# A new order table for a fused attention and channel-mix kernel: batch 6's q turned later, batch 7's k and v loaded side by side

## The chip, the cores and the metric

The kernel runs on one core of a Trainium2 chip. The time is the device time of one execution in microseconds (us). The engines that matter are TensorE (PE, with its weight loads PEld), VectorE (DVE), ScalarE (ACT), GpSimd (POOL) and SyncE (SP); the last two do little here but issue DMAs.

## The reference

Eight batches (B=8) with eight heads (H=8), 576 tokens (S=576), head size 64, so 512 channels; the hidden size F of the channel mix is 1024. The attention has no softmax: keys and values are first contracted into a 64 by 64 matrix for each head.

```python
kv  = einsum('bhsd,bhse->bhde', k, v)
o   = einsum('bhsd,bhde->bhse', q, kv)
o   = o / sqrt(mean(o * o, axis=-1) + 1e-6) * g_norm        # per head
x   = o.transpose(0, 2, 1, 3).reshape(B, S, 512)
xp  = x moved down by one token, zeros first                # token shift
xk  = mu_k * x + (1 - mu_k) * xp
xr  = mu_r * x + (1 - mu_r) * xp
kk  = relu(xk @ w_k)                                        # 512 -> 1024
out = sigmoid(xr @ w_r) * ((kk * kk) @ w_v)                 # 1024 -> 512
```

## The kernel before

The whole program is driven by a written table, ORDER (from line 18): eight strings ("periods") of words. A loop at the end of the kernel takes the words one after the other and calls the function that belongs to each. So the table sets, for every engine and every DMA queue, the order of its instructions. Each engine works through its own words in that order, and waits where a word needs something that is not there yet. A word has a name, numbers, and two marks:

- The digits behind `=` are the PSUM banks (of eight) that the word's result takes. A word that takes a bank waits until the one that held it before has been read out.
- A `'` at the end puts the word's elementwise part on DVE instead of ACT.

The words, by what they do for batch b:

- `ld.n.b` loads k (n=0), v (1) or q (2). POOL issues it (`load`, L196). Ahead of a load POOL copies one element of each DMA transpose that is still listed (L195), so a load, and all that POOL does after it, waits until every transpose that stands ahead of it in the table has landed.
- `kv` contracts k with v on PE (L288), `kvo` and `kvs` take the result out. `qt`/`qto` turn q on PE (batches 1 and 2), `qd` turns it by a DMA transpose that SP issues (from batch 3 on, L303). `u` multiplies q with kv (L354 or L318).
- `sq` (ACT, L359), `red` (DVE, L363), `nw` (DVE, eight small steps of a Newton iteration, L372 to L385) and `mul` (DVE, L423 or L401) are the norm. `mul` reads the last of u and so frees the bank of `u`.
- For batches 1 to 3 `x` and `x0` turn the normed result on PE (L438) and `xo`, `x0o` take it out. For batches 4 to 7 a DMA transpose does it (`yd`, SP, L411), and `gx` multiplies by g.
- `wrap`, `dif`, `sc` (L604 on ACT, L606 on DVE) and `add` (DVE, L621) make xk and xr.
- `K` is a half of a hidden block, four matmuls of 288 columns (L634) and a relu (L626 on ACT, L628 on DVE); `Kp` is the same in other sizes. `ks` and `ksp` square (L642 on DVE).
- `R` (four matmuls of 512 columns, L666) with the sigmoid on ACT; `V` (four, L676), two of them for a tile of 128 tokens; `fin` multiplies both on DVE (L689) and lets SP issue two stores (L699). `L` is the last tile.
- Batch 0 has words of its own so that PE can begin early, by pieces: `kvc`, `kvco`, `qtc`, `qtco` (out of PSUM, L217 on ACT, L219 on DVE), `uc`, `sqc` (square, L501), `msc` (mean by a matmul, L507), `rsc` (root, ACT, L511), `mcc` (product, DVE, L515), `difh`, `dih` (L598), `fu` (scale and add in one, DVE, L610), and `Ka`, `Kz`: the hidden blocks in two halves of the contraction (L725), `Ka` with the first two channel groups, `Kz` with the other two. Batch 1's attention is done in halves (`kvh`, L525, `uh`, L543, `sqh`, `redh`, `mulh`, `xh`, `x0h`).
- `wm.n.m` issues n matmuls on zeros (L261) between other work.

The periods overlap neighbouring batches: while the matmuls of batch b's channel mix run, the attention of b+1 and the transfers of b+2 go on. SP works through its transposes and stores strictly in the order of the table, and so does POOL through its loads.

Of the kernel before, what the change touches and what calls it, by code (L numbers as in the profile page):

```python
# [32 lines left out]
    Kp.0.1.2=1 rsh.5.9.0 mulh.1.1.0 sc.0.1.0 Kp.0.1.3=4 Vq.0.1.0=2 Vq.0.0.0=1 mulh.1.0.0 mulh.2.0.0 qt.1.1=70
    mulh.0.1.0 mulh.0.0.0 xh.2.2.0=36 x0h.0=54 qto.1.1.0 ld.2.3 xho.2.2.0.1 qto.1.1.1' x0ho.0.1' Vq.0.1.1
    xh.0.2.0=04 sc.0.1.1 xho.2.2.0.0' kvh.1=73 xho.0.2.0.0' kvho.1.1' ksp.0.1.4.8' Vq.0.0.1 kvho.1.0 uh.0.1=60
    uh.1.1=37 xho.0.2.0.1 uh.2.1=4 x0ho.0.0 Vq.0.0.2 sqh.0.1.1 sqh.1.1.1 sqh.0.0.1 sqh.1.0.1 ld.0.3 sqh.2.0.1
    add.0.1.1 Vq.0.3.0=5 Vq.0.3.1 redh.5.9.1 redh.0.5.1 rsh.5.9.1 rsh.0.5.1 Vq.0.1.2 mulh.0.1.1 mulh.0.0.1
    mulh.1.0.1 mulh.2.0.1 Vq.0.3.2 Vq.0.3.3 mulh.1.1.1 Vq.0.0.3 xh.2.2.1=06 Vq.0.1.3 xho.2.2.1.1 xho.2.2.1.0'
    xh.0.2.1=34 xho.0.2.1.0 x0h.1=76 add.0.1.0 Vq.0.2.0=0 xho.0.2.1.1 Vq.0.2.1 dif.1.384.576 tab R.0.1=3
    x0ho.1.1' wrap.1 x0ho.1.0' R.0.3=4 dif.1.0.384 sc.1.0.2.384.576' sc.1.0.3.0.384' sc.1.0.0.384.576' ld.1.3  # L40
    sc.1.0.2.0.384' sc.1.0.1.384.576' R.0.0=6 Vq.0.2.2 sc.1.0.1.0.384 qt.2.1=73 qt.2.0=46 ld.2.4 sc.1.0.0.0.384
    sc.1.1.3 sc.1.0.3.384.576' qto.2.1.1 Vq.0.2.3 fin.0.3 fin.0.0 R.0.2=5 adda.1.0.384.576 sc.1.1.1' qto.2.1.0
    Kp.1.0.2=1 add.1.0.1.0.384 Kp.1.0.0=3 add.1.0.0.0.384 qto.2.0.1' sc.1.1.2 sc.1.1.0 qto.2.0.0' fin.0.1
    Kp.1.1.2=5 add.1.1.1 Kp.1.1.3'=6 Kp.1.1.1'=7 Kp.1.1.4=4 add.1.1.0 fin.0.2 Kp.1.1.5=1 kv.2=32 Kp.1.1.0=5
    kvo.2.1' kvo.2.0' R.1.5=6 u.2.2=4 u.2.1=71 ksp.1.1.2.4' ksp.1.1.0.2' u.2.0=02 sq.2.1.1 ksp.1.1.4.6' sq.2.2.0
    Kp.1.0.3'=3 sq.2.1.0 qd.3 sq.2.0.0 sq.2.0.1 R.1.8=5 red.2.0.5 R.1.4=6 Kp.1.0.1=3 red.2.5.9 nw.2.0.1 nw.2.1.2
    nw.2.2.3 Kp.1.1.6=5 nw.2.3.4 Kp.1.1.7=6 nw.2.4.5 nw.2.5.6 nw.2.6.7 R.1.7=3 nw.2.7.8 mul.2.1.0 mul.2.1.1
# [7 lines left out]
    K.2.1.0=7 ld.2.5 nw.3.0.1 nw.3.1.2 K.2.5.1=5 nw.3.2.3 sc.2.1.2' nw.3.3.4 K.2.3.0=3 nw.3.4.5 nw.3.5.6
    nw.3.6.7 K.2.6.0=7 nw.3.7.8 K.2.6.1=5 K.2.2.0=3 K.2.2.1=7 sc.2.1.0' K.2.7.1=5 V.1.8.0=3 mul.3.0.1
    ks.2.3 ks.2.7 K.2.0.0=7 ks.2.0 mul.3.0.0 mul.3.1.0 mul.3.2.0 mul.3.1.1 K.2.4.1=0 add.2.1.0 K.2.4.0=5 x0.3=12
    ld.1.5 add.2.1.1 x.3.0.4=67 V.1.8.1 ks.2.2 xo.3.0.4.1 ks.2.1' x0o.3.0' ks.2.5 ks.2.4 R.2.0=4 ks.2.6'
    xo.3.0.4.0' R.2.2=0 x0o.3.1' wrap.3 dif.3 sc.3.0.2 sc.3.0.1 ld.0.5 V.2.0.0=5 ld.2.6 sc.3.0.0 V.2.0.1
# [8 lines left out]
    sc.3.1.3' K.3.1.1'=1 K.3.0.1=0 K.3.2.1=4 K.3.3.0=5 add.3.1.1 kvo.5.0' K.3.6.1'=7 ks.3.7 ks.3.2 fin.2.3
    kvs.5.0' ks.3.0 K.3.3.1=0 V.2.1.0=3 kvs.5.1 ks.3.5 R.3.7=4 V.2.1.1 u.5.1=51 ks.3.6' u.5.0=67 fin.2.1 ks.3.1'
    sq.5.1.0 u.5.2=0 sq.5.2.0 sq.5.1.1 sq.5.0.0 ks.3.3' sq.5.0.1 R.3.6=2 R.3.8=4 red.5.0.5 R.3.5=3 V.3.7.0=2  # L70
    gx.4.0 red.5.5.9 nw.5.0.1 gx.4.1' nw.5.1.2 nw.5.2.3 nw.5.3.4 R.3.4=4 nw.5.4.5 nw.5.5.6 nw.5.6.7 V.3.7.1
    V.3.4.0=3 wrap.4 nw.5.7.8 ld.0.6 dif.4 sc.4.0.2 mul.5.0.1 sc.4.0.0 sc.4.1.1 sc.4.0.1 sc.4.0.3 mul.5.2.0
# [14 lines left out]
    nw.6.7.8 mul.6.1.0 mul.6.0.0 K.5.1.0=6 V.4.0.1 sc.5.1.2 ks.5.2' kv.7=36 mul.6.1.1 kvo.7.1 kvo.7.0 qd.7
    add.5.1.0 V.4.1.0=2 V.4.1.1 kvs.7.1 mul.6.0.1 K.5.4.0=4 K.5.4.1=6 kvs.7.0' V.4.2.1 K.5.1.1=3 u.7.0=74
    mul.6.2.0 sq.7.0.0 yd.6 ks.5.7' sq.7.0.1 fin.4.0 add.5.1.1 u.7.1=50 u.7.2=6 sq.7.2.0 sq.7.1.0 R.5.4=3
    fin.4.2 sq.7.1.1 R.5.5=1 fin.4.1 ks.5.1' red.7.5.9 ks.5.3' red.7.0.5 nw.7.0.1 R.5.6=2 nw.7.1.2 nw.7.2.3  # L90
    R.5.8=3 nw.7.3.4 nw.7.4.5 ks.5.6 V.5.7.0=1 ks.5.4 nw.7.5.6 nw.7.6.7 V.4.3.0=2 nw.7.7.8 V.5.5.0=3 V.5.7.1
# [750 lines left out]
```

## Time and profile before

| | us |
|---|---|
| runs | 197.79, 198.43, 198.27 |
| median | 198.27 |
| profiled execution | 197.78 |
| its span | 196.0 |

| engine | busy us | share of the span |
|---|---|---|
| PE | 185.6 | 95% |
| PEld | 111.0 | 57% |
| DVE | 156.9 | 80% |
| ACT | 138.0 | 70% |
| POOL | 29.9 | 15% |

The profile is one execution; the profiled execution's own time is 1.8 us longer than the span of its instructions. In a row of the timeline stand: start, length, engine, line, operation, what is written from what is read, sizes, how many were joined, and in brackets the idle time ahead of it with what ended it. In a row of the windows stand: the stretch and its length, then for PE, PEld, DVE, ACT and POOL the busy time (and the number of instructions), the granted clock of PE, the DMA share and GB/s. In a row of the waits stand: total idle, how many times, the longest. A row of the chain has start and length. A row of the DMA issues ends with the time from the issue to the landing in us.

### The profile page before, as it was taken

The numbers are of one execution on the slowest core, as the hardware profiler recorded it, in microseconds if no ns is written. First come the engines' busy times: TensorE is split into PE (matmuls) and PEld (weight loads), VectorE is DVE, ScalarE is ACT, GpSimd is POOL, SyncE is SP. The second block draws the span as 40 slices with busy tenths as digits, with TensorE's granted clock in tenths as the row PEclk, the third lists the DMA queues.
The fourth block names the chain that finished last, engine by engine and source line by source line (L and its number), as shares of the span: only waits on it lengthen the run. The fifth ranks groups of instructions, "written<-read, shape, count | busy, mean of one in ns | idle before, by whom it ended". The sixth has DMA issues, their size and how long they took to land.

```text
span 196.0 us, 5662 instructions
## 1 busy us (share of the span) xinstructions
PE 185.6 (95%) x2314; PEld 111.0 (57%) x2343; DVE 156.9 (80%) x343; ACT 138.0 (70%) x285; POOL 29.9 (15%) x50
## 2 busy tenths in 40 slices
...
GB/s 213 213 210 207 198 207 205 208 223 260 215 184 169 131 246 212 210 271 177 149 185 135 215 128 184 247 229 5 181 120 118 127 54 0 107 3 109 107 158 163
DMA packets 42958, 32.75 MB, mean 167 GB/s; under 512 B 23852, under 2 KB 37428, under 8 KB 42932
## 3 DMA queue, kind: packets, MB, share of 16 engines
...
q8 instruction: 18, 0.29, 0.6%
...
HBM read 33.56 MB, written 9.44 MB: 219 GB/s over the span
## 4 chain that ended last, share of the span: by engine, by line
PE 64%; DMA 24%; DVE 6%; issue 2%; POOL 1%; ACT 1%; SPq 0%; POOLq 0%
PE ps_v L676 25%; PE ps_km L634 18%; DMA in_v<-in_v_dram 12%; PE ps_r L666 11%; DMA qT__1999<-in_q 7%; DMA rt<-in_v_dram 4%; PE ps_km L725 2%; PE ps_u L318 2%; DVE y__1672 L423 1%; DVE ss__1584 L363 1%; PE ps_warm L261 1%; PE ps_kv L288 1%; PE ps_v L684 1%; PE ps_x L438 1%; POOL q L183 1%
## 5 line engine op out<-in xcount | busy, mean ns | idle before, releaser
L676 PE MATMUL ps_v<-wv_sb,sqk 128*128 128x512 bf16 x264 | 65.1, 379 | 1.1 <-issue 0.5
L634 PEld LDWEIGHTS <-wk_sb 128*128 128x128 bf16 x480 | 45.9, 98 | 16.4
L676 PEld LDWEIGHTS <-sqk 128*128 128x128 bf16 x280 | 26.5, 98 | 28.3
L666 PE MATMUL ps_r<-wr_sb,xr 128*128 128x512 bf16 x134 | 34.7, 379 | 0.6 <-issue 0.2
L666 PEld LDWEIGHTS <-xr 128*128 128x128 bf16 x144 | 13.8, 98 | 14.3 <-DVE xr L621 0.2
L626 ACT ACTIVATE rt<-ps_km 128x384 bf16<-128x384 f32 (+2 forms) x20 | 9.5, 497 | 3.6 <-PE ps_km L634 1.9
L261 PE MATMUL ps_warm<-zeros 128*128 128x512 bf16 x25 | 9.1, 477 | 1.2 <-DVE eps L224 1.2
L634 PE MATMUL ps_km<-xk__3390,wk_sb 128*128 128x288 bf16 x64 | 9.0, 286 | 0.1
L634 PE MATMUL ps_km<-xk__2431,wk_sb 128*128 128x288 bf16 x64 | 8.8, 286 | 0.0
L634 PE MATMUL ps_km<-xk__2693,wk_sb 128*128 128x288 bf16 x64 | 8.7, 286 | 0.0
L634 PE MATMUL ps_km<-xk__986,wk_sb 128*128 128x192 bf16 (+1 forms) x64 | 8.5, 286 | 0.0
L634 PE MATMUL ps_km<-xk__3236,wk_sb 128*128 128x288 bf16 x64 | 8.5, 286 | 0.0
L634 PE MATMUL ps_km<-xk__1886,wk_sb 128*128 128x288 bf16 x64 | 8.4, 286 | 0.0
L634 PE MATMUL ps_km<-xk__1544,wk_sb 128*128 128x288 bf16 x64 | 8.2, 286 | 0.0
L428 ACT ACTIVATE xT<-ps_x,cols 128x256 bf16<-128x256 bf16 (+3 forms) x9 | 5.0, 591 | 2.8 <-PE ps_x L438 2.8
L261 PEld LDWEIGHTS <-zeros 128*128 128x128 bf16 x28 | 3.1, 116 | 5.5 <-issue 3.4
L725 PE MATMUL ps_km<-xk__376,wk_sb 128*128 128x320 bf16 x32 | 5.0, 299 | 0.5 <-DVE xk__376 L621 0.5
L428 ACT ACTIVATE xT<-xT,cols 128x1152 bf16<-128x1152 bf16 x4 | 5.0, 1261 | 0.0
L642 DVE TENSOR_TENSOR sqk<-rt 128x768 bf16<-128x768 bf16 (+2 forms) x7 | 4.5, 666 | 0.4 <-ACT rt L626 0.3
L628 DVE TENSOR_SCALAR rt__3521<-ps_km 128x288 bf16<-128x288 f32 x2 | 0.9, 458 | 4.7 <-ACT rt__3513 L626 4.7
L669 ACT ACTIVATE sig__3696<-ps_r 128x512 bf16<-128x512 f32 x1 | 0.6, 597 | 5.4 <-PE ps_r L666 5.4
L604 ACT ACTIVATE m__2398<-dx__2396,cols 128x576 bf16<-128x576 bf16 x4 | 2.9, 764 | 2.0 <-DVE dx__2396 L598 2.0
...
## 6 DMA issues: line engine op xcount, KB each, us to landing
q<-in_q_dram POOLq DMA_DIRECT2D x3, 576.0 KB, 18.5
sq<-in_k_dram POOLq DMA_DIRECT2D x3, 576.0 KB, 6.7
qT<-in_v_dram POOLq DMA_DIRECT2D x3, 576.0 KB, 11.2
in_q<-in_q_dram POOLq DMA_DIRECT2D x3, 576.0 KB, 13.0
in_k<-in_k_dram POOLq DMA_DIRECT2D x3, 576.0 KB, 18.5
in_v<-in_v_dram POOLq DMA_DIRECT2D x3, 576.0 KB, 18.0
...
sqk<-in_k_dram SPq DMA_DIRECT2D x1, 576.0 KB, 3.8
```

What stands on the lines that cost most here:

```text
L183: nc.gpsimd.dma_start(out=x_in[name, 0][:, ms], in_=by_token(dram[name], 0)[:, ms])
L261: nc.tensor.matmul(ps, zeros[:, :128], zeros, start=True, stop=True)
L288: nc.tensor.matmul(ps[e][half(i), M, :], kb[half(e), 2 * M + i, tok(j)], vb[half(e), 2 * M + i, tok(j)], start=(j == 0), stop=(j == G - 1))
L318: nc.tensor.matmul(out_, qT_[half(r), b // 2, half(ct % 2)], kv_[half(r), 0 if r == i else 1, ct, :], start=True, stop=True)
L428: eng.activation(out=dst, in_=src, func=AF.Copy, scale=g_sb)
L604: eng.activation(out=out_, in_=in_, func=AF.Copy, scale=mu)
L626: eng.activation(out=dst, in_=ps, func=AF.Relu)
L634: nc.tensor.matmul(ps[:, n, :], wk_sb[:, cc, 128 * fc:128 * fc + 128], at[b]["xk"][:, cc, c0:c1], start=(cc == 0), stop=(cc == NHP - 1))
L642: eng.tensor_mul(out=sqk[:, fcs, o:o + n], in0=src, in1=src)
L666: nc.tensor.matmul(ps, xr[:, cc, 128 * t:128 * t + 128], wr_sb[:, cc, :], start=(cc == 0), stop=(cc == NHP - 1))
L676: nc.tensor.matmul(ps, sqk[:, fc, 128 * t:128 * t + 128], wv_sb[:, fc, :], start=(fc == 0), stop=(fc == NFC - 1))
L725: nc.tensor.matmul(ps[:, n, :], wk_sb[:, cc, 128 * fc:128 * fc + 128], at[0]["xk"][:, cc, c0:c1], start=(cc == 0), stop=(cc == NHP - 1))
```

## The change

Only ORDER is replaced, all of it; no function is changed. Every step of the old table is in the new one, with the same number of matmuls. What differs is the order, the banks, the split of the warm matmuls, and the engine of some elementwise steps: 21 scales go from ACT to DVE and 16 the other way, 18 relus and 17 back, 14 squares and 9 back. In the parts that the text speaks of:

- Batch 0: `uc.1` now stands behind `qtc.2.2`; `kvco.2` between the two first `rsc`; `qtco.3'` behind `mcc.1`; `sc.0.0.0` on DVE; other banks for `Ka`. Seven `Ka` words stand ahead of the first `Kz` word and not five. `Kz.0.5` stands behind batch 1's `x0h.0`.
- Loads: batches 3 and 7 in another order (v3 ahead of k3; q7, k7, v7), k of batch 6 together with v of batch 6 behind `yd.4`.
- Transposes: `qd.5` behind `kv.5` (it stood right behind the `u` words of batch 4), and the two `fin` of batch 2 that stand ahead of it on SP in both tables are later too; `qd.6` behind `yd.5` (it stood ahead of it), just before the loads of batch 7 in the order that POOL sees.

Of the diff, the head and the places of the transposes:

```diff
-    qtc.2.2=70 msc.1=1
+    ... uc.0=5 qtc.2.2=67
-    ld.2.2 sqc.0 msc.0=3 qtco.2 rsc.0 wm.1.1=2 kvc.2.1=4 qtco.3' rsc.1 kvco.2' mcc.1 ...
-    ... mcc.0 rsc.2 uc.5=4 uc.3=1 difh.0.0.256.576 sqc.5 mcc.2 wm.3.4=7
-    msc.5=5 sc.0.0.1.256.576' dih.0.2.256.576 sqc.3 rsc.5 sc.0.0.0.256.576 sqc.4 msc.3=6 fu.0.0.2.256.576
-    add.0.0.0.256.576 wm.4.5=2 Ka.0.1=7 mcc.5 rsc.3 msc.4=3 Ka.0.7=2 mcc.3 dih.0.3.256.576 rsc.4 Ka.0.0=5
-    fu.0.0.3.256.576 wrap.0 mcc.4 Ka.0.2=6 difh.0.0.0.256 difh.0.1.0.256 fu.0.0.1.0.256 Ka.0.5=4 wm.2.6=3 Kz.0.5
-    ld.0.2 Kz.0.1 Kz.0.7 Ka.0.4=1 Kz.0.0' Kz.0.4 Ka.0.3=3 sc.0.1.3 Ka.0.6=0 Kz.0.2 Kz.0.6 qt.1.0=47 Kz.0.3
-    sc.0.1.2' wm.2.7=6 kvh.0=21 ...
+    sqc.0 uc.1=0 ld.2.2 sqc.1 qtco.2 msc.0=1 wm.2.1=4 msc.1=2 rsc.0 kvc.2.1=3 kvco.2 wm.2.2=6 uc.2=4 uc.4=6
+    rsc.1 mcc.1 qtco.3' mcc.0 difh.0.0.256.576 kvc.3.1=1 sqc.2 sqc.4 sc.0.0.1.256.576' sc.0.0.0.256.576' msc.2=3
+    kvco.3 wm.1.3=0 uc.3=2 msc.4=0 uc.5=1 sqc.3 rsc.4 msc.3=7 add.0.0.0.256.576 wm.4.4=5 Ka.0.0=5 rsc.3 sqc.5
+    mcc.3 Ka.0.5=0 rsc.2 dih.0.3.256.576 mcc.2 fu.0.0.3.256.576 mcc.4 msc.5=7 rsc.5 Ka.0.4=2 Ka.0.6=3 Ka.0.2=4
+    dih.0.2.256.576 fu.0.0.2.256.576 mcc.5 Ka.0.1=7 wrap.0 difh.0.0.0.256 Ka.0.7=6 difh.0.1.0.256 fu.0.0.3.0.256
+    Kz.0.4 Kz.0.0 Kz.0.1' Ka.0.3=1 Kz.0.3' fu.0.0.1.0.256 Kz.0.6 wm.2.5=5 qt.1.0=25 qto.1.0.1 Kz.0.2 Kz.0.7
+    fu.0.0.2.0.256 wm.2.6=1 kvh.0=37 ...
+    ld.1.2 Kp.0.1.2=1 mulh.1.1.0 xh.2.2.0=56 x0h.0=32 Kz.0.5 mulh.1.0.0 ...
...
-    ksp.1.1.4.6' sq.2.2.0 Kp.1.0.3'=3 ... red.2.0.5 ... red.2.5.9 nw.2.0.1 ...
-    V.1.4.0=5 ksp.1.1.6.8 mul.2.0.0 ksp.1.0.0.8 kv.3=63 V.1.5.0=7 V.1.5.1 mul.2.0.1 kvo.3.1 kvo.3.0' qd.4
-    mul.2.2.0 x.2.0.4=10 ...
+    ... red.2.0.5 R.1.4=4 red.2.5.9 Kp.1.1.6=7 Kp.1.0.1=2 R.1.5=4
+    ksp.1.1.4.6' ld.2.5 nw.2.0.1 V.1.5.0=7 ...
+    nw.2.5.6 nw.2.6.7 nw.2.7.8 mul.2.1.0 mul.2.1.1 V.1.5.1 mul.2.0.0 mul.2.0.1 kv.3=62 mul.2.2.0 ld.1.5 ld.0.5
+    ksp.1.0.0.8' x.2.0.4=31 ...
...
-    K.3.7.1'=4 u.4.2=0 sq.4.2.0 u.4.1=35 u.4.0=17 ... K.3.0.0'=6 qd.5 sq.4.0.0
-    ... kv.5=64 mul.4.0.1 yd.4 kvo.5.1 qd.6 ... ld.0.6 ... yd.5 ... ld.2.7 ... ld.1.7 ... ld.0.7
+    ... kv.5=20 mul.4.2.0 kvo.5.0 ks.3.0 qd.5 ... yd.4 ... ld.0.6 ... ld.1.6 ... yd.5 ...
+    add.4.0.0 qd.6 ... ld.2.7 ... ld.0.7 ... ld.1.7 ...
...
-    nw.6.2.3 nw.6.3.4 K.5.7.1=6 sc.5.1.1 V.4.0.0=0 ... nw.6.7.8 mul.6.1.0 mul.6.0.0 ... mul.6.1.1 ...
+    mul.6.0.1 R.5.6=4 K.5.5.0=0 V.4.0.0=6 kv.7=40 kvo.7.1 mul.6.1.1 K.5.5.1=3 mul.6.0.0 mul.6.1.0 ...
```

More of the change, by code (lines that the diff above doesn't have):

```diff
@@ L33 @@
[L33 to L47, printed above, removed]
@@ L55 @@
[L55 to L59, printed above, removed]
@@ L68 @@
[L68 to L72, printed above, removed]
@@ L87 @@
[L87 to L91, printed above, removed]
@@ L107 @@
-    ks.7.4 V.7.6.0=7 R.7.6=2 ks.7.7' fin.6.1 V.7.5.0=0 R.7.5=5 V.7.5.1 V.7.4.0=3 fip.7.5 V.7.7.0=4 V.7.4.1
-    fin.6.3 sta.7.5 fin.7.4 V.7.7.1 fip.7.7 V.7.6.1 R.7.8=6 sta.7.7 fip.7.6 sta.7.6 L.0=2 L.1=5
+    cast.1' cast.0 kvc.0.2=01 cols=2 kvco.0 qtc.0.2=34 kvco.1 qtco.0' qtco.1 wm.2.0=2 uc.0=5 qtc.2.2=67
+    """,
+    """
+    sqc.0 uc.1=0 ld.2.2 sqc.1 qtco.2 msc.0=1 wm.2.1=4 msc.1=2 rsc.0 kvc.2.1=3 kvco.2 wm.2.2=6 uc.2=4 uc.4=6
+    rsc.1 mcc.1 qtco.3' mcc.0 difh.0.0.256.576 kvc.3.1=1 sqc.2 sqc.4 sc.0.0.1.256.576' sc.0.0.0.256.576' msc.2=3
@@ new lines @@
+    uh.1.0=42 sqh.0.1.0 sqh.1.1.0 sc.0.1.3' uh.2.0=6 ksp.0.0.0.4' sqh.0.0.0 sqh.1.0.0 sqh.2.0.0 redh.5.9.0
+    redh.0.5.0 Kp.0.1.3=7 rsh.5.9.0 mulh.0.0.0 rsh.0.5.0 Kp.0.1.0=3 ld.0.2 Kp.0.1.1=7 mulh.0.1.0 mulh.2.0.0
+    ld.1.2 Kp.0.1.2=1 mulh.1.1.0 xh.2.2.0=56 x0h.0=32 Kz.0.5 mulh.1.0.0 x0ho.0.1 xh.0.2.0=74 ksp.0.1.0.4'
+    Vq.0.1.0=1 xho.0.2.0.0 sc.0.1.2 sc.0.1.0' xho.2.2.0.1' ksp.0.1.4.8' Vq.0.0.0=0 xho.0.2.0.1 xho.2.2.0.0'
+    qt.1.1=62 kvh.1=75 qto.1.1.1 Vq.0.1.1 kvho.1.0 x0ho.0.0' qto.1.1.0' kvho.1.1 Vq.0.0.1 uh.0.1=34 ld.2.3
@@ new lines @@
+    ksp.0.0.4.8' uh.1.1=62 uh.2.1=7 Vq.0.3.0=5 sqh.0.1.1 add.0.1.0 sqh.0.0.1 Vq.0.3.1 ld.1.3 add.0.1.1 sqh.1.1.1
+    sqh.2.0.1 sqh.1.0.1 redh.5.9.1 rsh.5.9.1 redh.0.5.1 rsh.0.5.1 Vq.0.3.2 tab ld.0.3 mulh.0.0.1 Vq.0.0.2
+    mulh.0.1.1 Vq.0.3.3 Vq.0.1.2 mulh.2.0.1 Vq.0.0.3 xh.2.2.1=34 mulh.1.1.1 mulh.1.0.1 xho.2.2.1.0' xho.2.2.1.1
+    Vq.0.1.3 xh.0.2.1=72 x0h.1=63 xho.0.2.1.0 xho.0.2.1.1 wrap.1 x0ho.1.0' x0ho.1.1' R.0.3=4 dif.1.384.576
+    dif.1.0.384 sc.1.0.3.384.576 R.0.2=6 sc.1.0.1.0.384' sc.1.0.2.384.576' sc.1.0.1.384.576 R.0.0=3 qt.2.0=72
@@ new lines @@
+    sc.1.1.0' qt.2.1=46 sc.1.0.3.0.384' sc.1.0.2.0.384' sc.1.0.0.0.384' qto.2.1.0 qto.2.1.1 sc.1.0.0.384.576'
+    R.0.1=3 adda.1.0.384.576 add.1.0.0.0.384 add.1.0.1.0.384 Kp.1.0.2'=4 qto.2.0.1' Kp.1.0.3'=6 Kp.1.1.1=3
+    Vq.0.2.0=4 ld.2.4 fin.0.1 Vq.0.2.1 fin.0.3 sc.1.1.1 add.1.1.0 Vq.0.2.2 Kp.1.1.2=2 qto.2.0.0' fin.0.0
+    sc.1.1.3' Vq.0.2.3 qd.3 sc.1.1.2' Kp.1.1.3'=6 Kp.1.1.0=3 Kp.1.1.5'=1 kv.2=57 ksp.1.1.0.2 kvo.2.0' kvo.2.1'
+    Kp.1.1.4=2 u.2.2=0 u.2.1=63 sq.2.2.0 add.1.1.1 sq.2.1.0 u.2.0=15 sq.2.1.1 Kp.1.0.0=7 sq.2.0.0 sq.2.0.1 qd.4
```

91 lines of the change are left out of this document (54 added, 37 removed).

## The prediction

> **What bounds the kernel now.** I read the page's head first, then the busy table cut at five places, then PE's waits, then the chain that ended last.
>
> ```profile
> span 196.0 us, 5662 instructions
> PE 185.6 (95%) x2314; PEld 111.0 (57%) x2343; DVE 156.9 (80%) x343; ACT 138.0 (70%) x285; POOL 29.9 (15%) x50
> ...
> 0.00:22.14 22.14, 18.34 (x259) 9.71 (x262) 12.31 (x36) 13.32 (x27) 13.71 (x26) 1.00 1.05 209
> 22.14:48.00 25.86, 25.23 (x447) 15.53 (x453) 23.95 (x58) 21.14 (x49) 5.18 (x7) 1.00 1.21 217
> 48.00:100.00 52.00, 50.22 (x802) 31.62 (x812) 47.08 (x100) 43.58 (x90) 6.07 (x9) 1.00 1.20 201
> 100.00:150.00 50.00, 49.69 (x555) 29.05 (x559) 46.54 (x98) 38.44 (x78) 4.92 (x8) 1.00 0.79 152
> 150.00:196.00 46.00, 42.15 (x256) 25.12 (x258) 27.05 (x55) 21.50 (x45) 0.00 (x0) 1.00 0.41 97
> ```
>
> TensorE (PE) is busy 185.6 of 196.0 us, at the full granted clock (1.00) in every stretch. Its idle time is 22.14 - 18.34 = 3.8 us in the head, 0.6, 1.8 and 0.3 us in the next three stretches, and 3.85 us in the last, nearly all behind the last matmul. The new table has the same matmuls, so it can move only the idle time, the gaps where PE changes shape, and the moment at which PE's steady work begins. DVE is the second bound: 46.54 of 50 us in the fourth stretch.
>
> ```profile
> PE ps_kv L288 <- DMA in_v<-in_v_dram: 0.4, 1, 0.4
> PE ps_u L318 <- DMA qT__1999<-in_q: 0.4, 1, 0.4
> ...
> PE 64%; DMA 24%; DVE 6%; issue 2%; POOL 1%; ACT 1%; SPq 0%; POOLq 0%
> ...
> 30.98 24.40 DMA in_v<-in_v_dram
> 83.15 14.58 DMA qT__1999<-in_q
> ```
>
> The chain calls DMA 24%. That is the length of the transfers on it, not what they cost: PE waited 0.4 us for v of batch 3 (issued 30.98, landed 55.38) and 0.4 us for the turned q of batch 5 (issued 83.15, landed 97.73). All that better transfers can give is 0.8 us. So the sum is made of the head, these two waits, and new waits on DVE.
>
> **The head (batch 0, words up to kvh.0).**
>
> ```profile
> 9.21 0.48 PE L484 MATMUL ps_qt<-ident,q 64*64 64x64 bf16 x36
> 9.23 0.87 ACT L501 ACTIVATE sq<-ps_u 128x384 bf16<-128x384 f32 x2 [0.30 <-PE ps_u L496]
> 10.52 1.07 ACT L511 ACTIVATE rs<-ps_ms,eps 128x384 f32<-128x384 f32 x2
> 12.81 0.21 ACT L217 CAST kv<-ps_kv 128x64 bf16<-128x64 f32 x1 [0.40 <-PE ps_kv L475]
> 9.78 0.46 DVE L219 COPY qT<-ps_qt 128x576 bf16<-128x576 bf16 x1 [0.91 <-PE ps_qt L484]
> 11.62 1.14 DVE L515 SCALAR_TENSOR_TENSOR xT<-ps_u,cols,rs 128x384 bf16<-128x384 f32 x2
> 12.79 0.49 DVE L598 TENSOR_TENSOR dx__357<-xT 128x640 bf16<-128x640 bf16 x1
> 14.23 0.29 DVE L606 TENSOR_SCALAR m__367<-dx__357,cols 128x320 bf16<-128x320 bf16 x1
> 15.53 0.49 DVE L621 TENSOR_TENSOR xk__376<-m__367,xT 128x640 bf16<-128x640 bf16 x1 [0.18 <-ACT m__367 L604]
> 17.11 0.33 DVE L598 TENSOR_TENSOR dx__357<-xT 128x320 bf16<-128x320 bf16 x1
> 17.47 0.55 DVE L610 SCALAR_TENSOR_TENSOR xk__376<-dx__357,cols,xT 128x320 bf16<-128x320 bf16 x1
> 18.12 2.88 PE L725 MATMUL ps_km<-xk__376,wk_sb 128*128 128x320 bf16 x20
> 14.63 1.02 PE L261 MATMUL ps_warm<-zeros 128*128 128x512 bf16 x4
> 22.14 0.36 PEld L525 LDWEIGHTS <-in_k 64*64 64x64 bf16 x36 [0.42 <-issue]
> ```
>
> Before, the two first roots on ACT end at 10.52 + 1.07 = 11.59, DVE then goes through its pieces, the last piece of xk (fu.3) ends at 17.47 + 0.55 = 18.02, and the first matmul of PE's second halves (Kz) starts 0.1 later, at 18.12. In the new table:
>
> - uc.1 stands behind the second qtc (the 9.21 row), so its matmul starts at about 9.65 and the second square at about 10.05 instead of 9.23 + 0.44 = 9.67: +0.4. Between the two roots stands kvco.2 on ACT: +0.2. The second root ends at about 12.2.
> - From there DVE has one chain to the last piece that the first Kz word needs, now fu.2: five products (mcc) at 0.57, the copy qtco.3 at 0.46 (before it lay in an idle gap at 9.78; now it is behind mcc.1), one wide difference 0.49, two scales 0.58 (one was ACT's before), the sum 0.49, two narrow differences 0.66, two fused pieces 1.10: 2.85 + 0.46 + 0.49 + 0.58 + 0.49 + 0.66 + 1.10 = 6.6. So fu.2 ends at about 18.8, and Kz starts at about 18.9, 0.8 us later.
> - The first Ka word, which needs add.0.0.0 only, can start a little sooner than now, but that does not carry: the next Ka words take the PSUM banks that mcc.3, mcc.2 and mcc.4 free, and these are links of the same chain. What is saved is that seven Ka words stand ahead of Kz and not five: two words of two matmuls, 2 x 2 x 0.144 = 0.58. Against it, four warm matmuls lie between Kz and kvh.0, and not two: 2 x 0.25 = +0.5. Kz.0.5 is taken from here to behind x0h.0: -0.3. kvh.0: 0.8 - 0.58 + 0.5 - 0.3 = +0.4.
> - Behind x0h.0, Kz.0.5 costs its 0.3 again, and stands alone between 64-row words, so PE changes shape once more: the 22.14 row shows 0.42 before such a change, an overlapped one less; taken 0.35. Up to uh.0.1 the lag is 0.4 + 0.3 + 0.35 = about 1.1. Ends: 0, if ACT and DVE find idle time that I do not see in the chain, and 1.6, if the products mulh.1.1.0 also arrive late (they stand one place later).
>
> PE has no idle time to take this up until 48 us: 25.86 - 25.23 = 0.6, all in gaps of shape. **Head: +1.1.**
>
> **Batch 2 and 3.**
>
> ```profile
> 58.05 0.70 PE L438 MATMUL ps_x<-ident,y__1270 64*128 64x64 bf16 x36
> 47.26 1.59 DVE L642 TENSOR_TENSOR sqk<-rt 128x768 bf16<-128x768 bf16 x3
> 50.22 2.60 DVE L363 TENSOR_REDUCE ss__1219<-sq__1193 128x20 f32<-128x1280 bf16 x2
> 54.67 2.48 DVE L423 TENSOR_TENSOR y__1270<-ps_u,rs__1240 128x512 bf16<-128x512 f32 x4
> 57.27 0.41 DVE L423 TENSOR_TENSOR y__1270<-ps_u,rs__1240 128x256 bf16<-128x256 f32 x1
> ```
>
> kv.3 moves behind the second half of V.1.5, and PE is 1.1 us late by then, while k and v of batch 3 are asked for about as before and in the other order: both have landed. **-0.40.** But DVE's chain to the flip x.2 (reductions 50.22 to 52.85, Newton steps to 54.67, products to 57.68) ended only 0.37 us before x.2 started, and that with PE held for 0.40. The new table puts one square, ksp.1.1.4.6, between the reductions and the Newton steps: 1.59 / 3 = 0.53, before it lay ahead of them. Then x.2 waits 0.40 + 0.53 - 0.37 = 0.56; a part is covered since another DVE step was taken out ahead of the reductions (a relu of Kp). **+0.45** (ends 0 and 0.9). So the first DMA wait comes back as a wait on DVE.
>
> **Batch 5's q (the "q turned" of the change).**
>
> ```profile
> 82.06 0.74 POOL L196 DMA_DIRECT2D qT<-in_v_dram  x1 [12.18 <-PE ps_kv L288]
> qT__1368<-q SPq DMA_TRANSPOSE x1, 5.3
> ```
>
> qd.5 goes to SP behind the stores of fin.2.0, and these products of DVE now stand behind u.4 and the sums of batch 3: I put its issue at about 87.7. Before, it ran beside loads (v of batch 6 was issued at 82.06) and landed 14.6 us after its issue; batch 4's, alone, took 5.3. In the new table the loads of k and v of batch 6 stand behind qd.5 and yd.4 and wait on POOL until both have landed, so only q of batch 6 can be beside it. By the row 5.3 it lands at 93, by 14.6 at 102.3; u.5 comes to PE at about 98.5 (97.78, where it was, with the terms above). I take the former end (no loads: 5 to 7.5 us). **-0.38**; at the other end +3.4.
>
> **Batches 6 and 7.**
>
> ```profile
> 109.17 3.33 SPq L411 DMA_TRANSPOSE xT<-yd  x1
> 114.44 0.26 POOL L195 COPY passed<-xT 1x2 bf16<-1x2 bf16 x1 [8.02 <-DMA xT<-yd]
> in_k<-in_k_dram POOLq DMA_DIRECT2D x1, 576.0 KB, 14.5
> 130.51 1.03 PE L676 MATMUL ps_v<-wv_sb,sqk 128*128 128x512 bf16 x4
> 131.38 0.65 PE L634 MATMUL ps_km<-xk__2693,wk_sb 128*128 128x288 bf16 x4
> 132.82 0.78 PE L288 MATMUL ps_kv<-in_v,in_k 64*64 64x64 bf16 x72
> ```
>
> qd.6 now stands behind yd.5, and the three loads of batch 7 wait on POOL for both. Queued behind that wait on POOL is nothing but these loads; who waits for them is kv.7. yd.5's issue at 109.17 + 1.1 of lag, 3.33 of issue, and 5.3 for qd.6: landed at 118.9, against 114.44 before. Three loads follow 0.7 us apart, the last (now v) at 120.6, and lands 14.5 later by the row of the last one before: 135.1. kv.7 came at 132.82; it is now 1.1 late and has about 2.2 us more PE work ahead of it (counted in V and R words of 131.38 - 130.51 = 0.87 and K words of about 0.5, four matmuls of a little under 0.144): 136.1. **0**, with 1.0 us to spare. k and v of batch 6 have some 5 us to spare by the same count.
>
> The Trainium skill, "DMA: Bandwidth & Descriptors", section "Anatomy of one DMA — SWDGE (gpsimd) path", gives one such transfer about 2.0 us plus its bytes over 436 GB/s; by that three loads of 1.18 MB would be in after an estimated 10 us, and kv.7 would have some 5 us to spare. The trace does not agree: the third took 14.5 us; the measured row stands in the sum above.
>
> V.4.0.0 takes the bank that mul.6.0.1 frees, the first product of batch 6 after both reductions and all Newton steps; before, it took a bank that a K word had left. DVE, 93% busy there, reaches it about when PE does: 0 (PE had 0.31 idle in that stretch) to 0.7 (one product later), taken **+0.35**. In the tail the last R, V and L words keep their order: 0.
>
> **Sum.** 1.1 - 0.40 + 0.45 - 0.38 + 0.35 = +1.1. The profiled execution took 197.78 us (span 196.0), the median of the runs is 198.27; 198.27 + 1.1 = 199.4, the profiled one about 198.9. About 0.3%, 0.6 us, can be told from no change here.
>
> **Rivals.**
>
> 1. *Faster: the head is not later.* The place is the start of Kz, the price its whole 1.1; it decides from kvh.0 at 22.2 or sooner. For it: Ka starts sooner, more Ka work is put ahead, and durations overstate a chain whose links overlap a little. Against: the copy and the scale added to a DVE that idles little there (0.18 in the 15.53 row). The two DMA waits then count: -0.78, and with x.2 covered 197.5.
> 2. *About even.* Half of the head's lag, x.2 and V.4.0.0 covered: 0.55 - 0.78 + 0.2, so 198.2.
> 3. *kv.7 waits for v of batch 7.* From a landing later than 15.5 us after its issue each us costs one. For: k and v of batch 7 are now the last thing that is asked for, behind two transposes. Against: a margin of 1.0. At 17.5 us it is +2: 201.4. A qd.5 that is held up as before gives more.
> 4. *The change does not do what it says:* the transfer of q lands no later than u.5 needs it in either table, so moving it can give 0.38 at most. That is part of my forecast.
>
> **Chances.** Forecast 0.50 (198.9 to 200.3), rival 3 and more waits on DVE 0.20, rival 2 0.13, rival 1 0.17. Faster by over 0.3% 0.17, within 0.13, slower 0.70. The range reaches from rival 1 to just above rival 3: 197.4 to 201.7.
>
> **What would show it.** Right: Kz's first matmul at 18.7 to 19.1, kvh.0 at 22.4 to 23.0, uh.0.1 (L543) 0.9 to 1.5 us later than before; no wait of PE for in_v or for qT of batch 5; a wait of L438 for the products of batch 2. Wrong: kvh.0 at 22.1, a wait of PE L288 for in_v behind 130, or PE idle for over 0.5 us at a place not named here.

## The result, and the profile after

The new table is faster: 197.39 us in the median of its runs against 198.15 for the table before, ratio 0.9957 (95% interval 0.9942 to 0.9972). I had forecast 199.4 with a range from 197.4. The time lies on the other side of no change, 0.01 us outside the range. One of the new table's eight runs took 200.53 us, at a lower granted clock (0.988), and is left out of the ratio. The profiled executions, 197.49 against 197.78, are only 0.3 us apart, since the one of before was the quickest of its eight runs; so the comparisons below go by medians and use the profiles for places.

The same views of the profile after: the busy table, cut at the same places, and an extract of PE's waits (total, times, longest).

```profile
0.00:22.14 22.14, 18.16 (x257) 9.43 (x260) 11.96 (x35) 11.82 (x25) 13.65 (x26) 1.00 1.05 210
22.14:48.00 25.86, 25.45 (x457) 15.38 (x459) 24.51 (x61) 19.15 (x47) 5.20 (x7) 1.00 1.22 209
48.00:100.00 52.00, 51.04 (x808) 31.84 (x811) 49.01 (x100) 42.96 (x94) 8.17 (x12) 1.00 1.12 201
100.00:150.00 50.00, 49.53 (x554) 28.97 (x560) 47.71 (x104) 35.01 (x70) 3.70 (x5) 1.00 0.86 158
150.00:195.70 45.70, 41.78 (x253) 24.87 (x255) 26.91 (x53) 24.90 (x47) 0.00 (x0) 0.99 0.41 96
...
PE ps_cols L588 <- DMA rows<-in_g_norm_dram: 0.7, 1, 0.7
...
PE ps_kv L475 <- DVE rt L219: 0.4, 1, 0.4
PE ps_ms L507 <- ACT sq L501: 0.3, 1, 0.3
PE ps_km L725 <- DVE xT L515: 0.3, 1, 0.3
PE ps_v L676 <- DVE out__3051 L689: 0.2, 1, 0.2
```

PE's idle time between 48 and 100 us fell from 1.8 to 1.0 us. The two waits for DMAs, in_v at kv.3 and the turned q of batch 5 at u.5, are gone from the list. The wait of 0.7 us for the rows of g_norm, at 8 us, is not in the list of before, and none of my terms has it. Against it, the wait just ahead of it (L475) fell from 1.0 to 0.4 us, and two of 0.3 for the loads of q and v there are gone; in the other kernels with the new head the wait for g_norm is 0.3 or not in the list. The chain that ended last shows the same of the two DMA waits, engine by engine:

```profile
PE 56%; DVE 30%; ACT 5%; issue 3%; DMA 3%; SPq 1%; DVEq 0%
```

The DMA share went from 24% to 3% (what is left is the load of g_norm at the start), and DVE's from 6% to 30%. This is again the length of the pieces on the chain and not what they cost: where PE waits for DVE in the list, it is 0.2 to 0.4 us each time, 1.2 at the warm-up. The four places that the prediction priced, in the timelines after (PE, DVE, SP and POOL; the row of in_v with 12.9 is from the list of DMA issues and ends with the time to landing):

```profile
17.99 0.55 DVE L610 SCALAR_TENSOR_TENSOR xk__371<-dx__326,cols,xT 128x320 bf16<-128x320 bf16 x1
18.59 1.79 PE L725 MATMUL ps_km<-xk__371,wk_sb 128*128 128x320 bf16 x12 [0.39 <-DVE xk__371 L610]
22.35 0.48 PE L525 MATMUL ps_kv<-in_v,in_k 64*64 64x64 bf16 x36
...
52.22 0.55 DVE L642 TENSOR_TENSOR sqk<-rt 128x768 bf16<-128x768 bf16 x1
54.56 2.82 DVE L423 TENSOR_TENSOR y__1281<-ps_u,rs__1252 128x512 bf16<-128x512 f32 x5
56.54 0.78 PE L288 MATMUL ps_kv<-in_v,in_k 64*64 64x64 bf16 x72
57.25 0.70 PE L438 MATMUL ps_x<-ident,y__1281 64*128 64x64 bf16 x36
...
85.72 5.62 SPq L303 DMA_TRANSPOSE qT__2157<-in_q  x1
96.42 0.98 PE L318 MATMUL ps_u<-kv__2078,qT__2157 64*64 64x64 bf16 x72
97.77 0.75 POOL L196 DMA_DIRECT2D sq<-in_k_dram  x1
98.50 0.75 POOL L196 DMA_DIRECT2D qT<-in_v_dram  x1
...
119.33 0.76 POOL L196 DMA_DIRECT2D in_v<-in_v_dram  x1
in_v<-in_v_dram POOLq DMA_DIRECT2D x1, 576.0 KB, 12.9
133.22 1.03 PE L676 MATMUL ps_v<-wv_sb,sqk 128*128 128x512 bf16 x4
134.18 0.78 PE L288 MATMUL ps_kv<-in_v,in_k 64*64 64x64 bf16 x72
```

kvh.0 starts 0.21 us later than before (22.35 against 22.14). kv.3, the flip x.2 right behind it, and u.5 start with no idle time ahead of them: their rows have no bracket. V.4.0.0 (133.22) and kv.7 (134.18) do not wait either.

### The profile page after: what moved, and what is told of

It is laid out like the page before. It is cut to its first block, busy times and chain, and to the rows that moved or that the text cites. A ratio compares the mean times of both kernels' runs of the same rounds, so it can differ in the third digit from the quotient of the medians.

```text
span 195.7 us, 5668 instructions
## 1 busy us (share of the span) xinstructions
PE 186.0 (95%) x2316; PEld 110.5 (56%) x2343; DVE 160.1 (82%) x349; ACT 133.8 (68%) x279; POOL 30.7 (16%) x50
## 4 chain that ended last, share of the span: by engine, by line
PE 56%; DVE 30%; ACT 5%; issue 3%; DMA 3%; SPq 1%; DVEq 0%
PE ps_km L634 21%; PE ps_v L676 17%; PE ps_r L666 11%; DMA rows<-in_g_norm_dram 3%; DVE yd L401 3%; DVE sqk L642 2%; DVE xr L621 2%; PE ps_kv L288 1%; DVE y__1281 L423 1%; PE ps_km L725 1%; DVE xT L515 1%; DVE ss__1215 L363 1%; PE ps_u L318 1%; DVE ss__2860 L363 1%; DVE ss__1583 L363 1%
## 5 line engine op out<-in xcount | busy, mean ns | idle before, releaser
L676 PE MATMUL ps_v<-wv_sb,sqk 128*128 128x512 bf16 x265 | 64.4, 379 | 1.4 <-issue 0.8
L666 PE MATMUL ps_r<-wr_sb,xr 128*128 128x512 bf16 x135 | 35.2, 379 | 0.6
L626 ACT ACTIVATE rt<-ps_km 128x384 bf16<-128x384 f32 (+2 forms) x18 | 8.8, 506 | 7.0 <-PE ps_km L634 4.2
L634 PE MATMUL ps_km<-xk__3239,wk_sb 128*128 128x288 bf16 x64 | 9.0, 286 | 0.0
L634 PE MATMUL ps_km<-xk__2666,wk_sb 128*128 128x288 bf16 x64 | 8.8, 286 | 0.0
L634 PE MATMUL ps_km<-xk__3386,wk_sb 128*128 128x288 bf16 x64 | 8.7, 286 | 0.1
L634 PE MATMUL ps_km<-xk__2429,wk_sb 128*128 128x288 bf16 x64 | 8.7, 286 | 0.0
L634 PE MATMUL ps_km<-xk__1923,wk_sb 128*128 128x288 bf16 x64 | 8.7, 286 | 0.0
L634 PE MATMUL ps_km<-xk__1557,wk_sb 128*128 128x288 bf16 x64 | 8.4, 286 | 0.1
L428 ACT ACTIVATE xT<-xT,cols 128x1152 bf16<-128x1152 bf16 x6 | 7.3, 1266 | 0.1
L515 DVE SCALAR_TENSOR_TENSOR xT<-ps_u,cols,rs 128x384 bf16<-128x384 f32 x6 | 3.7, 613 | 3.1 <-ACT rs L511 3.1
L195 POOL COPY passed<-xT 1x2 bf16<-1x2 bf16 x2 | 1.3, 672 | 27.5 <-DMA xT<-yd 27.4
L195 POOL COPY passed<-qT__1198 1x2 bf16<-1x2 bf16 x1 | 1.5, 1532 | 22.9 <-DMA qT__1198<-q 22.9
L642 DVE TENSOR_TENSOR sqk<-rt 128x1280 bf16<-128x1280 bf16 (+3 forms) x7 | 5.1, 722 | 0.0
```

Source lines behind the costliest of these rows:

```text
L428: eng.activation(out=dst, in_=src, func=AF.Copy, scale=g_sb)
L515: DVE.scalar_tensor_tensor(out=xT[0][:, hps, P + c0:P + c1], in0=give(("uc", key)), scalar=g_sb, in1=rs0[:, hps, c0:c1], op0=ALU.mult, op1 ...
L626: eng.activation(out=dst, in_=ps, func=AF.Relu)
L634: nc.tensor.matmul(ps[:, n, :], wk_sb[:, cc, 128 * fc:128 * fc + 128], at[b]["xk"][:, cc, c0:c1], start=(cc == 0), stop=(cc == NHP - 1))
L642: eng.tensor_mul(out=sqk[:, fcs, o:o + n], in0=src, in1=src)
L666: nc.tensor.matmul(ps, xr[:, cc, 128 * t:128 * t + 128], wr_sb[:, cc, :], start=(cc == 0), stop=(cc == NHP - 1))
```

## The experiments

All are the kernel of before or after with words of the table moved; the functions are the same, and no kernel leaves work out. Their tables are written in fewer lines, so L in their rows lies 21 lower than above (L267 is kv's L288, L297 is u's L318). "Ratio" is against runs of the table before on the same chip.

**First: which transfer was worth what, and the head.** kv.3 alone, to its place in the new table, with the words around it: the product mul.2.2.0, the flip x.2 and kv.3's readouts change places too, and x0.2 takes another bank:

```diff
-  kv.3=63 V.1.5.0=7 V.1.5.1 mul.2.0.1 kvo.3.1 kvo.3.0' qd.4 mul.2.2.0 x.2.0.4=10 x0.2=26 xo.2.0.4.1
+  V.1.5.0=7 V.1.5.1 mul.2.0.1 mul.2.2.0 kv.3=63 qd.4 x.2.0.4=10 kvo.3.1 x0.2=24 xo.2.0.4.1 kvo.3.0'
```

> The table of before with one place changed: kv.3 stands behind V.1.5.1, right ahead of the flip x.2, as in the new table (its readout kvo.3 moves with it, x0.2 takes bank 4 instead of 6). Theory A: the new table's gain is the two DMA waits (kv.3, u.5) and one change of PE's shape at x.2. Then PE's wait for in_v (0.40) goes, x.2 follows kv.3 without a gap of its own (0.42 before), and the time falls by 0.6 to 0.8 us. Prediction's step: x.2 waits for the products of batch 2 and gives the 0.40 back: 0 to -0.2. Rival B, the gain lies in the later batches' order: -0.2 at most.

Measured: 197.73, ratio 0.9984 (0.9972 to 0.9997): 0.3 us by the ratio, 0.4 by the medians, about half of what theory A gave. And one word later only, between the two halves of V.1.5:

```diff
-  kv.3=63 V.1.5.0=7
+  V.1.5.0=7 kv.3=63
```

> The table of before with kv.3 one word later, between V.1.5.0 and V.1.5.1: 0.86 us later on PE, but not beside x.2. Theory A: the wait for in_v (0.40) goes and the change of shape stays: -0.3 to -0.45, half of what kv.3 beside x.2 gives. If only the wait counts, both kernels are alike.

Measured: 198.12, ratio 1.0000 (0.9987 to 1.0014). The wait for in_v is gone and nothing is won: its profile shows PE waiting 1.0 us at u.5, where before waited 0.4. The load beside that transfer:

```diff
-  kvo.4.0 ld.1.6 kvo.4.1 ...   yd.4 kvo.5.1
+  kvo.4.0 kvo.4.1 ...          yd.4 ld.1.6 kvo.5.1
```

> The table of before with the load of v of batch 6 moved from ahead of kv.4's end to behind yd.4 (so behind qd.5, which then runs beside fewer loads). Theory A: the turned q of batch 5 lands in 5 to 9 us instead of 14.6, u.5's wait (0.38) goes: -0.3 to -0.45, and the spread of the runs becomes smaller if this wait is what varies. Rival: the transpose is slowed by something else, the wait stays: 0.

Measured: 197.40, ratio 0.9968 (0.9958 to 0.9978): 0.7 us, nearly twice the wait that the profile of before shows. The transpose of batch 5's q, issued at 83.10, landed 12.0 us later, at 95.1, and not after 14.6 at 97.7; PE reached u.5 at 97.26 without a wait. Its 11 runs lie between 197.20 and 197.64 where the 33 of before lay between 197.26 and 198.69. Last, the new table with the head of before, joined at uh.0.1:

> The new table with the head of before: all words up to uh.0.1 in the order of before, then the new table (banks renamed at the joint). Theory A: the new head costs 0.46 us at uh.0.1, so this runs 0.4 to 0.5 faster than the new table and 1.1 to 1.3 faster than before. Prediction's step: the head costs 1.1, so 1.1 faster than the new table. Rival: the head's lag is taken up later by DVE's waits, no difference from the new table (-0.76 against before).

Measured: 197.57, ratio 0.9978 (0.9962 to 0.9994). No gain over the new table (0.9957), but the joint itself is at fault in part: PE led by 0.4 us at uh.0.1 (30.42 against 30.83) and had lost that at xh.0.2.1 (35.25 against 35.24), which waited for DVE, whose words of the two tables lie differently there. The kernel does not tell what the head costs.

**Second: are the two waits in series?** The load put back in the new table, as early as before:

```diff
-  kvo.4.0 kvs.4.0 ...          V.3.4.0=7 ld.1.6 mul.5.1.1
+  kvo.4.0 ld.1.6 kvs.4.0 ...   V.3.4.0=7 mul.5.1.1
```

> The new table with one load moved back: v of batch 6 right behind kvo.4.0, as early as in the table of before, so ahead of qd.5. Theory A (the load beside the transpose is what holds it up): the turned q of batch 5 lands 10 to 15 us after its issue at 86 instead of 8, at 96 to 101, and u.5, which comes at 96.4, waits 0.5 to 4 us: 1 to 3 us slower than the new table. Theory A' (only the k load and the copies matter): no difference. Rival B (the place of the gain is elsewhere): no difference.

Measured: 198.67, ratio 1.0020 (1.0008 to 1.0032). This one load takes the new table from 0.9957 to above 1. Then kv.3 and the load together, with V.1.5.0 in a bank that does not wait for DVE:

```diff
-  kv.3=63 V.1.5.0=7 V.1.5.1 ... x0.2=26
+  V.1.5.0=3 V.1.5.1 mul.2.0.1 mul.2.2.0 kv.3=67 qd.4 x.2.0.4=10 kvo.3.1 x0.2=24     (and ld.1.6 behind yd.4)
```

> The table of before with v of batch 6 behind yd.4, and kv.3 behind V.1.5.1 right ahead of the flip x.2, with V.1.5.0 in bank 3 so that it doesn't wait for the products of batch 2 (with bank 7 it waited 0.3 in the kernel with kv.3 alone). Theory A, with u.5's transfer as the point that takes in all that is gained ahead of it: without the transfer's wait the 0.40 and one change of PE's shape (0.3) come through, so 0.5 to 0.7 faster than with the load moved alone (197.40), 1.2 to 1.4 faster than before. Rival: DVE is the bound from u.2 on and gives it back: like the load moved alone.

Measured: 196.28, ratio 0.9906 (0.9892 to 0.9920). This is quicker than both tables; it is called the quickest table below. And the same place of kv.3 without the load moved:

> kv.3 behind V.1.5.1 and V.1.5.0 in bank 3, the load of batch 6's v left as early as in the table of before. With both edits the time was 0.9906 of before, with the load alone 0.9968, so the place of kv.3 gave 1.1 us there. Theory A (the two waits stand in series: u.5 waits until the transfer lands, whenever PE comes): nearly all of the 1.1 is given back at u.5, whose wait grows from 0.4 to 1.2 or more; 0 to -0.4 against before. Rival (the gains add): -1.1, 0.994.

Measured: 197.87, ratio 0.9989 (0.9975 to 1.0004). So the same edit gives 1.1 us where u.5 does not wait and 0.2, which the interval does not tell from nothing, where it does. The rows of u.5 show how. First the four kernels with the early load: the table before, kv.3 to the new place, the same with the other bank, the new table with the early load; then the two with the late load, kv.3 in the old place and in the new.

```profile
97.78 0.86 PE L318 MATMUL ps_u<-kv__2081,qT__1999 64*64 64x64 bf16 x72 [0.38 <-DMA qT__1999<-in_q]
98.28 0.86 PE L297 MATMUL ps_u<-kv__2081,qT__1999 64*64 64x64 bf16 x72 [0.77 <-DMA qT__1999<-in_q]
98.18 0.86 PE L297 MATMUL ps_u<-kv__2081,qT__1999 64*64 64x64 bf16 x72 [1.72 <-DMA qT__1999<-in_q]
97.37 0.92 PE L297 MATMUL ps_u<-kv__2079,qT__2158 64*64 64x64 bf16 x72 [1.07 <-DMA qT__2158<-in_q]
...
97.26 0.86 PE L297 MATMUL ps_u<-kv__2080,qT__1998 64*64 64x64 bf16 x72
95.96 0.86 PE L297 MATMUL ps_u<-kv__2080,qT__1998 64*64 64x64 bf16 x72
```

In the two with kv.3 moved (second and third row) u.5 starts at 98.2 to 98.3 although PE comes there at 97.5 and at 96.5. Whatever is won ahead of u.5 turns into a longer wait at u.5. Only without the early load does it start when PE comes, at 96.0 in the quickest.

Between the last two rows PE's lead can be followed: 0.73 us at V.1.7.0 (59.65 against 60.38), of which 0.54 is the wait at kv.3's old place and about 0.15 a change of PE's shape that is saved; 1.12 at the V words behind x.3 (73.48 against 74.60), where x.3 no longer waits 0.18 for DVE; 1.3 at u.4 and u.5. (The profile puts that wait of kv.3 down to ACT; the load of v of batch 3 landed at 55.3 and kv.3 started at 55.47.)

**The head by its mirror.** The new table up to kv.2, then the table of before with ld.1.6 behind yd.4; and once more with kv.3's place as in the quickest:

> The mirror: the new table up to kv.2, then the table of before, with v of batch 6 behind yd.4 so that no transfer hides the head. Against the table of before with that load moved alone (197.40, 0.9968 of before): theory A: 0.4 to 0.6 slower, so 0.999 to 1.0 of before. Prediction's step: 1.1 slower, 1.002. Rival, the head's lag is taken up: 0.997.

> The best table so far with the new table's order for all words up to kv.2. The new head made no difference where kv.3 still waited for its load (0.9961 against 0.9968), though PE lagged 0.4 us at uh.0.1 and up to 0.9 later. Theory A (kv.3's wait took the lag in): here, with no transfer that PE waits for, the head costs 0.4 to 0.9: 196.7 to 197.2. Rival (DVE takes it in between u.3 and x.3): 196.3 to 196.5. Prediction's step: +1.1, 197.4.

Measured: 197.27, ratio 0.9961 (0.9946 to 0.9976), against 0.9968 with the head of before: no cost. And 197.16, ratio 0.9958 (0.9945 to 0.9971), against 0.9906: 0.9 us of cost. The new head costs where PE waits for nothing behind it, and costs nothing where kv.3 stands waiting for its load anyway: in the first kernel PE was 0.52 us late at kv.2 (46.07 against 45.55), 0.90 at V.1.4.0 (54.81 against 53.91), 0.30 behind kv.3, whose wait of 0.54 is gone, and 0.07 at u.5. The 0.9 has the joint in it: Kp.1.0.0 and R.1.5 lie ahead of u.2 here and behind it in the new table. By these places about 0.5 of it is the head, which ends at kv.2, and 0.4 the joint. The other way round, the new table with the head of before up to kv.2:

> The new table with the order of before for all words up to kv.2 (three words of the new table's part follow it, then the new table, banks renamed). Theory A: PE lags 0.61 us at kv.2 in the new table, so this is 0.4 to 0.6 faster than the new table. Prediction's step: 1.1 faster. Rival: DVE is the bound between u.2 and the products of batch 2 and later, no difference from the new table.

Measured: 198.37, ratio 1.0018 (1.0006 to 1.0030), slower by 1.0. PE led the new table by 0.84 us at kv.2 (45.50 against 46.34) and lost it at the joint, in part by a wait of u.2 for DVE and one of 0.54 for a relu on ACT that holds a bank:

```profile
47.89 1.05 PE L333 MATMUL ps_u<-kv__1056,qT__886 64*64 64x64 bf16 x40 [0.20 <-DVE kv__1056 L198]
51.75 0.82 PE L613 MATMUL ps_km<-xk__986,wk_sb 128*128 128x192 bf16 x8 [0.54 <-ACT rt L605]
```

It tells of the joint, not of the head. kv.2 itself can be compared over all the profiles: with the head of before it starts at 45.50 to 45.85 (nine kernels), with the new head at 46.03 to 46.56 (six) and at 47.08 in the second kernel of the mirror, whose profiled run was its slowest. So the new head brings PE to kv.2 some 0.5 us later. How much of that reaches the end of the new table stays open.

**The later place of qd.6.**

```diff
-  yd.4 ... yd.5 ... add.4.0.0 qd.6
+  yd.4 qd.6 ... yd.5
```

> The new table with qd.6 ahead of yd.5, right behind yd.4, as in the table of before; the loads' order is left. The prediction gave the later qd.6 no cost, with 1.0 us to spare at kv.7; the trace shows v of batch 7 landed 1.9 us ahead of kv.7. Expected: the three loads of batch 7 are no longer held by qd.6, and k and v of batch 6 are (qd.6 now stands ahead of them); 0, at most 0.3 either way. Rival (kv.7 waits in many runs): 0.5 or more faster.

Measured: 198.03, ratio 1.0005 (0.9990 to 1.0020): 0.6 us slower than the new table by the medians (0.9 by the ratios), which none of the expectations had. The place is kv.6 and not kv.7. POOL and PE in this kernel:

```profile
101.68 0.20 POOL L174 COPY passed<-qT__2203 1x2 bf16<-1x2 bf16 x1 [32.15 <-DMA qT__2203<-q]
102.67 0.74 POOL L175 DMA_DIRECT2D sq<-in_k_dram  x1 [0.32 <-issue]
103.40 0.76 POOL L175 DMA_DIRECT2D qT<-in_v_dram  x1
...
111.97 0.78 PE L267 MATMUL ps_kv<-qT,sq 64*64 64x64 bf16 x72 [0.72 <-DMA qT<-in_v_dram]
```

With qd.6 ahead of them k and v of batch 6 also wait until qd.6 has landed: they are issued at 102.7 and 103.4 instead of 97.8 and 98.5, and PE waits 0.72 us for v.

**Third: the terms of the prediction by themselves.** The place of the square, on the quickest table:

```diff
-  ksp.1.1.2.4' ksp.1.1.0.2' u.2.0=02 sq.2.1.1 ksp.1.1.4.6' ... red.2.5.9 nw.2.0.1
+  ksp.1.1.2.4' ksp.1.1.0.2' u.2.0=02 sq.2.1.1 ... red.2.5.9 ksp.1.1.4.6' nw.2.0.1
```

> The best table so far (196.28) with the square ksp.1.1.4.6 between the reductions and the Newton steps of batch 2, as in the new table; before, it stood ahead of the reductions. Prediction's step: the flip x.2 waits for the products, 0.45 slower. Theory A: the flip reads only the first four products, not the last (mul.2.2.0), and the square is only moved within DVE's own queue, its work ahead of the products is the same: 0 to 0.1.

Measured: 196.24, ratio 0.9899 (0.9884 to 0.9914): no cost. One V word between kv.3 and the flip x.2, on the quickest table and on the new one:

```diff
-  V.1.5.1 ... kv.3 ... x.2.0.4 ... V.1.4.1
+  V.1.5.1 ... kv.3 V.1.4.1 ... x.2.0.4 ...
```

> The best table so far (kv.3 moved, load of v of batch 6 behind yd.4; 196.28) with V.1.4.1 between kv.3 and the flip x.2, so that PE changes its shape once more; nothing else. Theory A: 0.3 to 0.45 slower than 196.28, as the gap before x.2 was 0.42 and fell to 0.04 beside kv.3. Rival (the gap is not a cost of its own, DVE sets x.2's place): no difference.

> The new table with V.1.4.1 between kv.3 and the flip x.2. Theory A: one more change of PE's shape, 0.3 to 0.6 slower than the new table (197.39), so 0.998 to 0.9995 of before. Rival: DVE takes it in on the way to x.3: 197.4.

Measured: 196.89, ratio 0.9944 (0.9923 to 0.9964), and 198.14, ratio 0.9995 (0.9983 to 1.0007): 0.6 and 0.7 us slower. Both are more than theory A gave (0.3 to 0.45 and 0.3 to 0.6), and the cause is another. The quickest table first, then the one with V.1.4.1 between:

```profile
56.57 0.78 PE L267 MATMUL ps_kv<-in_v,in_k 64*64 64x64 bf16 x72
57.28 0.70 PE L417 MATMUL ps_x<-ident,y__1270 64*128 64x64 bf16 x36
58.13 0.81 PE L655 MATMUL ps_v<-wv_sb,sqk 128*128 128x512 bf16 x3 [0.16 <-issue]
58.78 1.03 PE L645 MATMUL ps_r<-wr_sb,xr 128*128 128x512 bf16 x4
...
56.56 0.78 PE L267 MATMUL ps_kv<-in_v,in_k 64*64 64x64 bf16 x72
57.49 0.81 PE L655 MATMUL ps_v<-wv_sb,sqk 128*128 128x512 bf16 x3 [0.16 <-issue]
58.24 0.70 PE L417 MATMUL ps_x<-ident,y__1270 64*128 64x64 bf16 x36
59.34 1.02 PE L645 MATMUL ps_r<-wr_sb,xr 128*128 128x512 bf16 x4 [0.41 <-DVE xT L409]
```

The order itself costs 59.34 - 0.41 - 58.78 = 0.15 us. The other 0.41 is a wait for DVE's readout of the flip, which holds the bank of R.1.6; the flip itself came 0.96 later (58.24 against 57.28). So the flip's time is what counts: DVE's work on batch 2 begins with it. In the new table a K word waits 0.20 us for a bank that DVE holds, at 65.73; where the rest of its 0.7 arises is not shown.

Last, Kz.0.5 put back ahead of kvh.0 in the new table:

```diff
-  Kz.0.2 Kz.0.7 ... x0h.0=32 Kz.0.5
+  Kz.0.2 Kz.0.7 Kz.0.5 ... x0h.0=32
```

> The new table with Kz.0.5 back among the other Kz words, ahead of kvh.0. Prediction's step: the shape change that Kz.0.5 makes behind x0h.0 costs 0.35, so this is 0.35 faster. Theory A: PE would stand there anyhow, waiting for the products of batch 1's first half (gaps of 0.21 and 0.26 in place of 0.42), so the place costs at most 0.1: within 0.15 of the new table.

Measured: 197.44, ratio 0.9962 (0.9950 to 0.9975), the new table's own within the interval. The place of Kz.0.5 costs nothing that can be seen: with it ahead of kvh.0, kvh.0 starts at 22.63 and not at 22.35, PE then waits 0.31 us for a square on DVE, and uh.0.1 comes 0.28 later than in the new table (31.11 against 30.83), where I had counted 0.35 earlier.

## Why the prediction was wrong, point by point

- **u.5's transfer: -0.38. Right in mechanism, mis-sized.** I priced the wait by the idle time of one execution. But this wait stands behind all the others, and the landing hardly depends on when PE and DVE let the transpose go: with the load moved it landed at 94.3 to 95.2 in nine kernels that issued it between 81.8 and 87.3 (at 92.1 and 92.3 in the two of the mirror), with the early load at 97.3 to 98.3 for issues between 82.2 and 86.6. So the wait hides every gain ahead of it, and every loss up to its own length. The 5.3 us that I took for the transfer was too short: in the kernels made from the new table with the late load it took 7.6 to 9.1. It landed ahead of u.5 all the same, so I was on the right side. Moving the load alone gave 0.7 us (0.9968), and putting it back into the new table cost 1.3. The Trainium skill, "DMA: Bandwidth & Descriptors", section "Queues, rings and completion order", says that a DMA engine takes the queue rows in turns, packet by packet; the delay by a load on another queue (14.6 us from issue to landing with it, 12.0 with only that load moved) agrees with that, though no run here shows the packets' turns. A sum that adds up terms ahead of u.5 and then the wait itself has to ask first whether the wait stays.
- **kv.3 and x.2: -0.40 + 0.45. The step that failed, and the largest error of the sum, is the return at x.2.** Together I gave the two +0.05; measured, kv.3's place gave -1.1. I counted the product mul.2.2.0 in the chain of the flip. The flip reads only the four products ahead of it, so it had 58.05 - 57.15 = 0.9 us of room and not 0.37, and the square in the middle moves no work in or out ahead of the products: alone it cost nothing (196.24 against 196.28). The return exists, at another place: with V.1.5.0 in bank 7 PE waited 0.3 for DVE's products there. The new table has another bank. The place of kv.3 was worth 1.1 us where u.5 didn't wait (0.9906 against 0.9968), not 0: 0.54 of it was PE's wait at kv.3, about 0.15 the saved change of shape, and the rest appears behind the flip, where DVE's work on batch 2 comes earlier.
- **Head: +1.1. Right sign, about half the size.** fu.2 ended at 17.99 + 0.55 = 18.54 and not at 18.8; kvh.0 came 0.21 late and not 0.4; uh.0.1 0.45 (30.83 against 30.38) and not 1.1; kv.2 0.61. Kz (18.59) and kvh.0 (22.35) thus came just ahead of the windows that were to show me right, and uh.0.1 well ahead of its own. The term of 0.35 for Kz.0.5 was wrong: ahead of kvh.0 it would have made uh.0.1 0.28 later, for the wait for DVE's square. By the mirror the head with its joint is worth 0 or 0.9, depending on what waits behind it, and the head alone some 0.5.
- **V.4.0.0: +0.35. Wrong.** No wait: the row at 133.22 has no bracket, and PE idles 50.00 - 49.53 = 0.47 in that whole stretch.
- **qd.6 and batch 7: 0. Half right.** kv.7 has the room that I gave it: v of batch 7, issued at 119.33, took 12.9 us, so it landed at 132.2, 1.9 ahead of kv.7, where I gave 1.0. The Trainium skill, "DMA: Bandwidth & Descriptors", section "Anatomy of one DMA — SWDGE (gpsimd) path", gives one such load 2.0 us plus its bytes over 436 GB/s, an estimated 10 us for three together; the 14.4 us from the first one's issue (117.86) to the last landing do not agree. But I asked only what the later qd.6 does to the loads behind it, and not what it sets free ahead of it: k and v of batch 6. Its old place costs 0.6.
- **Rivals.** The first had the right side and nearly the time (197.5), with x.2 covered and the two DMA waits counted. Its reason, a head that isn't later, is not what happened: the head is later, and kv.3's place gave more than it counts. That its time is so near is luck.

Put together by medians: 198.1, the load -0.7, kv.3's place -1.1, the new head +0.9 make 197.2, and 196.8 with 0.5 for the head without the joint; the new table has 197.39. These 0.2 to 0.6 stay open. The signs of the two gains were in the prediction. What turned the sum is that both were priced by the idle time of one profile, 0.78 us together against 1.8 measured, and that 0.80 of new waits (0.45 at x.2, 0.35 at V.4.0.0) was added that are not there.
